# Decode attention with a gated MLP: whole batches in place of half batches, and half of the first key block turned on VectorE

## The chip, the cores and the metric

The kernel runs on one core of a Trainium2 chip. The core has a matrix engine (PE, TensorE), a vector engine (DVE, VectorE), an activation engine (ACT, ScalarE), a general engine (POOL, GpSimd) and a queue engine (SP, SyncE), and 16 load engines (DMA) that bring data from the chip's memory (HBM) into the on-chip buffer (SBUF). Matmul results land in a small accumulation memory (PSUM). Each engine works through its own instructions in order and waits on semaphores for the others. The metric is device time in microseconds; the kernel before takes 194.29 us (median of three runs, 194.04 to 194.38).

## What is computed

Eight sequences each decode one token of 448 features. An attention over the last 1024 cached positions (16 query heads, 8 key heads, 256 features a head) and an MLP (448 to 1792 to 448) run on the same token, and a sigmoid gate mixes them:

```python
q = (x @ wq).reshape(B, Sq, Hq, Dh).transpose(0, 2, 1, 3)
k = repeat(k_cache[:, :, Sk - W:, :], 2, axis=1)      # W = 1024
v = repeat(v_cache[:, :, Sk - W:, :], 2, axis=1)
p = softmax(einsum("bhqd,bhkd->bhqk", q, k) * Dh ** -0.5)
a = einsum("bhqk,bhkd->bhqd", p, v).transpose(0, 2, 1, 3).reshape(B, Sq, Hq * Dh) @ wo
h = gelu(layernorm(x) @ w1 + b1)
b = h @ w2 + b2
g = sigmoid((x * gate_w).sum(-1, keepdims=True))
return g * a + (1 - g) * b
```

All inputs are bfloat16. The used part of each cache is 33.5 MB; the weights add 10.6 MB.

## The kernel before

**Units.** A unit `u` is half a batch: 4 key heads of one sequence, 2 MB of keys and 2 MB of values; there are 16 units. One load puts a unit into a ring slot of 16 KB a partition: partition `32a + s` holds key head `a` and positions `32s` to `32s + 31`, so a partition reads one run of 16 KB. Only the first key load is cut in two pieces of 1 MB, with runs of 8 KB.

**The ring.** `plan` lists the loads in the order they are issued on SP: keys 0, w1, wq in two slots, w2, then keys and values in turn (values three units behind, `LAG`), and wo. The ring has `RING` = 9 slots. `pump()` issues loads while there are slots, and `done()` after the last use of a slot lets one more be issued; the load into a slot waits on the engine that read it last. Small inputs (x, gate weights, biases) are loaded on ACT's queue.

**A unit's work.** `transpose_keys(u)` turns the keys so that features lie on partitions: 32 PE transposes of 128x128 four-byte words (two bfloat16 each) into PSUM, four to a PSUM tile `ktp`, of which there are three; each tile is copied to `kt` in SBUF, four by ACT and four by VectorE (L349, L351). `scores(u)` does 32 matmuls into `S_ps`, one group of 32 partitions per key head; `top` takes the maximum on VectorE (L407). `expo`, `turn` and `bring` (exponential on ACT, 32x32 block transposes on VectorE, a permutation matmul) are called between the PSUM tiles of the next unit's transposes: `steps(u)` names after which. `values` does 16 matmuls into `PO`, and `finish` adds the parts with a small matmul and writes the head outputs to `oT`.

**Ends.** `norm_and_gate` comes first (layer norm of x, the gate, both turned on PE), then the transposes of unit 0, the MLP's hidden layer (`mlp_hidden`, 70 matmuls with w1 as the stationary operand), the queries, and the first scores. At the end `spread_rows` and `project` multiply the attention output with wo in 128 matmuls of 112 columns, and four stores write the result.

**Order.** The order is written by hand (`manual_schedule`); engines take their instructions as the functions are called. Waits follow from the tiles and from the pools: a tile of a pool with `bufs` buffers waits until a buffer's former tile is no longer read.

Of the kernel before, what the change touches and what calls it, by code (L numbers as in the profile page):

```python
# [17 lines left out]
def kernel(  # L18
# [15 lines left out]
    nc = tc.nc  # L34
# [10 lines left out]
    assert (NB, Sq, D, Hkv, Dh, Hq, W, F) == (8, 1, 448, 8, 256, 16, 1024, 1792)  # L45
    NJ = Dh // P
    NC = W // P
# [3 lines left out]
    NF = F // P  # L51
    FH = F // 2
    HH = HD // 2
    PAIR = 2
    OT = 4
    DO = D // OT
    QN = 512
    QUAD = 4
    RQ = QUAD * rep
    NQ = NB * Hkv // QUAD  # L60
    SK = P // QUAD
    NCK = W // SK
    NH = 2
    CH = NCK // NH
    SLOT = 8192
    CB = NC // NJ
    HPQ = 4
    NHQ = Hq // HPQ
    NJ8 = HPQ * NJ
    WO_PARTS = [[(0, NJ8)]] * (NHQ - 1) + [[(0, 4), (4, 6), (6, 8)]]  # L70
    RING = 9
    LAG = 3
    BIG = 1e30
# [8 lines left out]
    ktpool = ctx.enter_context(tc.tile_pool(name="ktpool", bufs=4))  # L82
    epool = ctx.enter_context(tc.tile_pool(name="epool", bufs=2))
    opool = ctx.enter_context(tc.tile_pool(name="opool", bufs=LAG + 1))
# [8 lines left out]
    consumed = [0]  # L93

# [10 lines left out]
    def kv_loader(src, u, parts):  # L105
        b, half = divmod(u, Hkv // QUAD)
        v = src[b, half * QUAD : (half + 1) * QUAD, kv_base:Sk, :].rearrange(
            "a (s c) d -> s a (c d)", c=NCK
        )

        def load(t):
            n = NCK * Dh // parts
            for i in range(parts):
                nc.sync.dma_start(  # L114
                    t[:, i * n : (i + 1) * n], v[:, :, i * n : (i + 1) * n]
                )

        return load

    def rows_loader(pieces):  # L120
        def load(t):
            o = 0
            for ap in pieces:
                n = 1
                for s in ap.shape[1:]:
                    n *= s
                dst = t[:, o : o + n]
                if len(ap.shape) == 3:
                    dst = dst.rearrange("p (a n) -> p a n", a=ap.shape[1])
                nc.sync.dma_start(dst, ap)  # L130
                o += n

        return load

    index = {}

    def add(key, loader):
        index[key] = len(plan)
        plan.append(loader)

    def add_kv(name, src, u, parts=1):
        add((name, u), kv_loader(src, u, parts))
# [5 lines left out]
    w2_v = B_w2.rearrange("(p c) n -> p (c n)", c=NF)  # L148
    wo_v = A_wo.rearrange("(q p j) n -> p q (j n)", p=P, j=NJ8)

    add_kv("k", A_k_cache, 0, parts=2)
    add(("w1",), rows_loader([w1_m, w1_t]))
    add(("wq", 0), rows_loader([wq_m[:, 0 : 2 * HD]]))
    add(("wq", 1), rows_loader([wq_m[:, 2 * HD : 3 * HD], wq_t]))
    add(("w2",), rows_loader([w2_v]))
    for u in range(1, NQ):
        add_kv("k", A_k_cache, u)
        if u >= LAG:
            add_kv("v", A_v_cache, u - LAG)
    for u in range(NQ - LAG, NQ):  # L160
        add_kv("v", A_v_cache, u)
    for q in range(0, NHQ, 2):
        add(
            ("wo", q),
            rows_loader(
                [
                    wo_v[:, q + i, j0 * D : j1 * D]
                    for i in range(2)
                    for j0, j1 in WO_PARTS[q + i]
                ]  # L170
            ),
        )

    def slot(*key):
        return slots[index[key]]

# [3 lines left out]
    gw_b = consts.tile([NB, D], BF16)  # L180
    b2_r = consts.tile([1, D], BF16)
    b1_sb = consts.tile([P, NF], BF16)
    nc.scalar.dma_start(
        gw_b[:], gate_w.rearrange("(o d) -> o d", o=1).to_broadcast([NB, D])
    )
    nc.scalar.dma_start(b2_r[:], B_b2.rearrange("(o d) -> o d", o=1))
    nc.scalar.dma_start(b1_sb[:], B_b1.rearrange("(p c) -> p c", c=NF))

# [4 lines left out]
    ones_f = consts.tile([P, P], F32)  # L193
    nc.gpsimd.memset(ones_f[:], 1.0)
# [3 lines left out]
    PO = ps_po.tile([P, PAIR, Dh], F32)  # L198
    nc.vector.memset(PO[:], 0.0)

    NX = NR + 2

    def tiles(ps):
        return [
            (ps[32 * i : 32 * i + NB, :], slice(i * DO, (i + 1) * DO))
            for i in range(OT)
        ]

    xz = consts.tile([NB, 2, P], BF16)
    yz = consts.tile([NB, 2, P], BF16)  # L210
    nc.vector.memset(xz[:], 0.0)
    nc.vector.memset(yz[:], 0.0)
    xT = consts.tile([P, NX, NB], BF16)
    yT = consts.tile([P, NX, NB], BF16)
    sel = consts.tile([P, RQ], F32)
    sel2 = consts.tile([P, RQ], F32)
    own = consts.tile([P, PAIR], F32)
    qw = consts.tile([P, NJ, NB, Hq // RQ, QUAD, RQ], BF16)
    oT = consts.tile([P, Hq, NJ, NB], BF16)
    gg = consts.tile([NB, 2], F32)  # L220
    spread = consts.tile([NB, OT, P // OT], F32)
    gg_s = consts.tile([P, 2], F32)
    ones_r = consts.tile([1, NB], BF16)
    mixb = consts.tile([P, DO], F32)
    res = consts.tile([P, DO], BF16)
    nc.vector.memset(spread[:], 0.0)
    nc.vector.memset(ones_r[:], 1.0)

    def transposed(dst, src, srcz):
        tp = ps_misc.tile([P, NX, NB], BF16, tag="misc", name="tp")  # L230
        for r in range(NR):
            nc.tensor.transpose(tp[:, r, :], src[:, r:DM:NR], ident[:NB, :NB])
        for h in range(2):
            nc.tensor.transpose(tp[:, NR + h, :], srcz[:, h, :], ident[:NB, :NB])
        nc.vector.tensor_copy(dst[:], tp[:])

    for h in range(2):
        nc.vector.tensor_copy(xz[:, h, h::2], x_sb[:, DM:D])
    transposed(xT, x_sb, xz)
    nc.vector.reduce_sum(  # L240
        sel[:], ident[:].rearrange("p (a s) -> p s a", a=QUAD)[:, 0:RQ, :], axis=AXIS.X
    )
    halfs = ident[:].rearrange("p (a s) -> p s a", a=QUAD)
    for i in range(PAIR):
        nc.vector.reduce_sum(
            own[:, i : i + 1], halfs[:, i * RQ : (i + 1) * RQ, :], axis=AXIS.XY
        )
    nc.vector.reduce_sum(
        sel2[:],
        ident[:]  # L250
        .rearrange("p (a h s) -> p s a h", a=QUAD, s=RQ)[:, :, :, 0:PAIR],
        axis=AXIS.XY,
    )
    perm = consts.tile([P, P], BF16)
    nc.vector.tensor_copy(
        perm[:].rearrange("p (s a) -> p s a", a=QUAD),
        ident[:].rearrange("p (a s) -> p s a", a=QUAD),
    )
    cap = consts.tile([P, 1], F32)
    rows = consts.tile([P, 1], F32)  # L260
    for a in range(QUAD):
        nc.vector.reduce_sum(
            rows[32 * a : 32 * a + 32, :],
            ident[32 * a : 32 * a + 32, (32 + rep) * a : (32 + rep) * a + rep],
            axis=AXIS.X,
        )
    nc.vector.tensor_scalar(
        cap[:], rows[:], 2.0 * BIG, -BIG, op0=ALU.mult, op1=ALU.add
    )
    nc.vector.memset(qw[:], 0.0)  # L270

    def norm_and_gate():
# [18 lines left out]
        for h in range(2):  # L291
            nc.vector.tensor_copy(yz[:, h, h::2], y_sb[:, DM:D])
        transposed(yT, y_sb, yz)
# [6 lines left out]
            in1=gw_b[:],  # L300
# [5 lines left out]
        nc.scalar.activation(gth[:], gl[:], ACT.Tanh, scale=0.5)  # L306
        nc.vector.tensor_scalar(
            gg[:, 0:1], gth[:], 0.5, 0.5, op0=ALU.mult, op1=ALU.add
        )
        nc.vector.tensor_scalar(  # L310
            gg[:, 1:2], gth[:], -0.5, 0.5, op0=ALU.mult, op1=ALU.add
        )
        nc.vector.tensor_copy(
            spread[:, :, 0:NB],
            ident[0:NB, 0:NB]
            .rearrange("p (o b) -> p o b", o=1)
            .to_broadcast([NB, OT, NB]),
        )
        gp = ps_misc.tile([P, 2], F32, tag="misc", name="gp")
        nc.tensor.matmul(  # L320
            gp[:],
            lhsT=spread[:].rearrange("p i b -> p (i b)"),
            rhs=gg[:],
# [3 lines left out]
        nc.vector.tensor_copy(gg_s[:], gp[:])  # L327

    KT = {}
    def transpose_keys(u, between=None):  # L330
        kn = slot("k", u)[:].bitcast(F32)
        between = between or {}
        for hf in range(NH):
            kt = ktpool.tile([P, QUAD, CH, SK, NJ], BF16, tag="kt", name="kt")
            KT[hf] = kt
            for i in range(CH // CB):
                c0 = i * CB
                g = hf * (CH // CB) + i
                ktp = ps_kt.tile([P, CB, P, NJ], BF16, tag="ktp", name="ktp")
# [12 lines left out]
                for step in between.get(g, ()):  # L352
                    step()
# [209 lines left out]
    for u in range(1, NQ):  # L563
        transpose_keys(u, steps(u - 1))
        if u >= LAG:
            values(u - LAG)
# [94 lines left out]
```

## Time and profile before

| What | Value |
|---|---|
| Median of three runs | 194.29 us |
| Span of the profiled execution, first to last instruction | 192.9 us (the page gives no further time for it) |
| Busy: PE, VectorE, ACT, POOL | 141.4, 121.4, 84.3, 1.3 us |
| Loads | 77.90 MB in 6737 packets, mean 404 GB/s |
| Mean granted PE clock | 0.907 of full |
| Chain that ended last | 96% loads |

The profile shows one execution. Its second part cuts the span into 40 slices of 4.8 us and gives, for each, an engine's busy tenths, the PE clock that was granted and the rate of the loads. The chain of waits goes back from the last instruction, at each step to what released it. A group's row gives the source line, engine, operation, output and input tiles, shapes, count, then total busy time and the mean of one in nanoseconds, then the idle time ahead of it and what ended most of that. In the list of waits a row gives the engine, what it waited for, total, times and longest in us; `SPq` and `ACTq` are the queues on which loads are issued. In a table of stretches, a row gives from and to, the length, the busy time and count of PE, PE's weight loads, VectorE, ACT and POOL, then the PE clock, the load engines' share and GB/s.

### The profile page before, as it was taken

Reading aid. Unit: us, or ns where it says so; the run is one execution under the profiler, and the core shown is the slowest. Engines: PE = TensorE matmul, PEld = TensorE weight load, DVE = VectorE, ACT = ScalarE, POOL = GpSimd, SP = SyncE. Lnnn points to the kernel's source line nnn. Section 1 sums busy time; section 2 is a strip of 40 time slices with the busy share of each in tenths; the row PEclk is TensorE's granted clock in tenths of the full one; section 3 lists DMA queues with packets and bytes.
Section 4 is the critical chain, followed back from the end, with each engine's and each line's share of the span. In section 5 each row is a group of like instructions: output and inputs, shape, how many; then the busy total and the mean of one; then the engine's idle time right before and its main releaser. Section 6 shows DMA issues by size and latency. Waiting matters only on the chain.

```text
span 192.9 us, 3529 instructions
## 1 busy us (share of the span) xinstructions
PE 141.4 (73%) x1478; PEld 104.7 (54%) x1478; DVE 121.4 (63%) x278; ACT 84.3 (44%) x102; POOL 1.3 (1%) x9
## 2 busy tenths in 40 slices
PE   1299957788888859797858586869786978935671
PEld 0199526465575649484636363739473948612360
DVE  7632335797987848576858676765867584863310
ACT  2343024587583817182818182827282725520000
POOL 2000000000000000000000000000000000000000
PEclk9999699999999997969999999996999696995558
DMA  5999999999999999999999999999999999999960
GB/s 173 426 427 415 429 440 423 404 431 431 431 431 421 425 418 425 435 426 428 425 418 431 416 431 428 428 428 421 428 428 421 428 431 425 428 418 413 417 240 7
DMA packets 6737, 77.90 MB, mean 404 GB/s; under 512 B 945, under 2 KB 1346, under 8 KB 1986
## 3 DMA queue, kind: packets, MB, share of 16 engines
q1 hardware_dynamic: 6512, 77.67, 95.5%
q8 instruction: 11, 0.18, 0.4%
q10 hardware_dynamic: 210, 0.02, 0.2%
q14 instruction: 4, 0.03, 0.0%
HBM read 77.68 MB, written 0.01 MB: 403 GB/s over the span
## 4 chain that ended last, share of the span: by engine, by line
DMA 96%; SPq 1%; issue 0%; DVE 0%; PE 0%
DMA slot<-in_A_k_cache_dram 58%; DMA slot<-in_A_v_cache_dram 21%; DMA slot<-in_A_wo_dram 10%; DMA slot<-in_A_wq_dram 7%; SPq L114 1%; SPq L130 1%; DVE res L620 0%; PE A_ps L604 0%
## 5 line engine op out<-in xcount | busy, mean ns | idle before, releaser
L343 PE MATMUL ktp<-ident_f,slot 128*128 128x128 f32 x512 | 78.0, 306 | 24.3 <-DMA slot<-in_A_k_cache_dram 16.0
L349 ACT COPY kt<-ktp 128x1024 bf16<-128x1024 bf16 x64 | 63.2, 1016 | 71.2 <-PE ktp L343 71.1
L343 PEld LDWEIGHTS ktp<-ident_f,slot 128*128 128x128 f32 x512 | 64.7, 157 | 33.6 <-issue 16.2
L351 DVE COPY kt<-ktp 128x1024 bf16<-128x1024 bf16 x64 | 41.8, 686 | 27.5 <-PE ktp L343 27.5
L423 DVE STREAM_TRANSPOSE EB<-E 128x1024 bf16<-128x1024 bf16 x16 | 19.9, 1243 | 5.9 <-ACT E L415 5.9
L407 DVE TENSOR_REDUCE nmx<-S_ps 128x1 f32<-128x1024 f32 x16 | 19.5, 1219 | 3.3 <-PE S_ps L395 3.3
L456 PE MATMUL PO<-slot,ET 128*16 128x512 bf16 x256 | 18.3, 410 | 2.1 <-DMA slot<-in_A_v_cache_dram 2.1
L395 PE MATMUL S_ps<-kt,qw 128*8 128x512 bf16 x256 | 18.2, 388 | 1.4 <-ACT kt L349 1.1
L415 ACT ACTIVATE E<-S_ps,nmx 128x1024 bf16<-128x1024 f32 x16 | 17.9, 1119 | 2.4 <-DVE nmx L408 2.4
L395 PEld LDWEIGHTS <-qw 128*8 128x8 bf16 x256 | 7.1, 85 | 8.8 <-issue 2.1
L456 PEld LDWEIGHTS <-ET 128*16 128x16 bf16 x256 | 5.4, 91 | 8.7 <-issue 5.4
L436 DVE CAST ET<-sm 128x256 bf16<-128x256 f32 x16 | 6.6, 415 | 0.7 <-PE sm L434 0.7
L434 PEld LDWEIGHTS sm<-selr,ones_f 128*128 128x128 f32 x32 | 5.0, 198 | 0.6 <-issue 0.4
L484 DVE CAST oT<-sm 128x16 bf16<-128x16 f32 x16 | 3.5, 219 | 2.9 <-PE sm L481 2.9
L434 PE MATMUL sm<-selr,ones_f 128*128 128x8 f32 x32 | 4.8, 222 | 0.0
L431 PE MATMUL sm<-EB,perm 128*128 128x256 bf16 x16 | 4.5, 279 | 0.3 <-DVE oT L484 0.3
L604 PE MATMUL A_ps<-slot,oP 128*8 128x112 bf16 x128 | 3.5, 273 | 1.1 <-DMA slot<-in_A_wo_dram 1.1
L514 DVE TENSOR_TENSOR z<-hT,b_sb 128x112 f32<-128x112 f32 x1 | 0.3, 274 | 5.5 <-PE hT L504 5.5
L604 PEld LDWEIGHTS <-oP 128*8 128x8 bf16 x128 | 2.7, 114 | 1.8 <-issue 1.8
L415 ACT ACTIVATION_READ_ACCUMULATOR E<-S_ps,nmx 128x1 f32 x16 | 3.2, 202 | 0.0
L363 PE MATMUL S_ps<-slot,xT 128*8 128x512 bf16 x32 | 3.2, 576 | 0.0
L438 DVE RECIPROCAL rb<-sm 128x8 f32<-128x8 f32 x16 | 3.2, 198 | 0.0
(145 smaller groups left out, 82.5 us busy)
## 6 DMA issues: line engine op xcount, KB each, us to landing
slot<-in_A_v_cache_dram SPq DMA_DIRECT2D x16, 2048.0 KB, 38.1
slot<-in_A_k_cache_dram SPq DMA_DIRECT2D x15, 2048.0 KB, 37.5
slot<-in_A_wo_dram SPq DMA_DIRECT2D x3, 896.0 KB, 31.8
slot<-in_A_k_cache_dram SPq DMA_DIRECT2D x2, 1024.0 KB, 7.4
slot<-in_A_wq_dram SPq DMA_DIRECT2D x1, 2048.0 KB
slot<-in_B_w_dram SPq DMA_DIRECT2D x1, 1568.0 KB
slot<-in_B_w_dram SPq DMA_DIRECT2D x1, 1344.0 KB, 10.1
slot<-in_A_wq_dram SPq DMA_DIRECT2D x1, 1024.0 KB
```

Source lines behind the costliest of these rows:

```text
L343: nc.tensor.transpose(words[:, c, :, 0], kn[:, o : o + P], ident_f[:])
L349: nc.scalar.copy(dst, src)
L351: nc.vector.tensor_copy(dst, src)
L395: nc.tensor.matmul(S_ps[32 * a : 32 * a + RQ, hf * CH * SK : (hf + 1) * CH * SK], lhsT=qw[:, j, b, half, a, :], rhs=KT[hf][:, a, :, :, j], ...
L407: nc.vector.reduce_max(nmx[:], S_ps[:], axis=AXIS.X, negate=True)
L415: nc.scalar.activation(E[:], S_ps[:], ACT.Exp, bias=nmx[:], scale=1.0, accum_out=rowsum[:])
L423: nc.vector.transpose(EB[:].rearrange("p c r -> p (c r)"), E[:])
L431: nc.tensor.matmul(sm[:, 0:NCK, :], lhsT=perm[:], rhs=EB[:, :, 0:RQ], start=True, stop=True)
L434: nc.tensor.matmul(sm[:, NCK, :], lhsT=ones_f[:], rhs=selr[:], start=True, stop=True)
L436: nc.vector.tensor_copy(ET[:], sm[:, 0:NCK, :])
L456: nc.tensor.matmul(PO[32 * t : 32 * t + PAIR * RQ], lhsT=ET[:, PAIR * c : PAIR * (c + 1), :], rhs=vn[:, PAIR * c * Dh : PAIR * (c + 1) * D ...
L604: nc.tensor.matmul(dst, lhsT=oP[:, j, q, :], rhs=w[:, o + cols.start : o + cols.stop], start=(q == 0 and j == 0), stop=(q == NHQ - 1 and j ...
```

## The change

The unit becomes a whole batch: 8 key heads, 4 MB of keys, two loads of 2 MB into one slot of 32 KB a partition, and the ring has 4 slots. wq takes one slot, w1 and w2 share one, wo takes one. The order of loads is keys 0, wq, w1 with w2, keys 1, then values and keys in turn, and wo. Each of `S_ps`'s groups of 32 partitions now holds four rows of scores, for two key heads, so a batch has one maximum and one exponential. The exponential writes four-byte floats and is turned together with its row sums; the scale 1/sum and the gate are multiplied in at once, and a mask made from the identity puts each head's weights in its columns. `softmax(b)` is called right after `scores(b)`, and then `values(b - 1)`, `bring(b)`, `finish(b - 1)`; nothing is called between the transposes any more. `finish` turns and adds on VectorE, without PE.

x, y, the queries and the MLP's hidden values are turned with VectorE's block transposes and small copies instead of PE transposes; biases and gate weights come as single rows and are spread by VectorE's shuffle. The MLP and projection matmuls have x and the attention output as stationary operand and the weights as moving operand with 448 (or 224) columns. Two stores write the result.

The first half of the keys of batch 0 (`turn_blocks(0, 0)`) is not turned by PE: VectorE turns it in 32x32 blocks into a tile `B`, and 16 copies of 32 partitions by 2048 elements, 6 on VectorE, 7 on ACT, 3 on POOL, bring the blocks to their partitions. `kt` and `B` share a pool of two buffers. TensorE has 2235 instructions for 2987.

```diff
-    SLOT = 8192
-    RING = 9
-    LAG = 3
+    HS = NCK * Dh
+    SLOT = NG * HS
+    RING = 4
+    EARLY = 16
-    ktpool = ctx.enter_context(tc.tile_pool(name="ktpool", bufs=4))
+    ktpool = ctx.enter_context(tc.tile_pool(name="ktpool", bufs=2))
...
+    add(("k", 0), kv_loader(A_k_cache, 0))
+    add(("wq",), rows_loader([wq_m, wq_t]))
+    add(("w12",), rows_loader([w1_m, w1_t, w2_v]))
+    add(("k", 1), kv_loader(A_k_cache, 1))
+    for b in range(2, NB):
+        add(("v", b - 2), kv_loader(A_v_cache, b - 2))
+        add(("k", b), kv_loader(A_k_cache, b))
...
+    for t in range(QD):
+        nc.scalar.dma_start(
+            b1_r[BL * t : BL * t + 1, :],
+            B_b1[FQ * t : FQ * (t + 1)].rearrange("(o d) -> o d", o=1),
+        )
...
+    nc.vector.stream_shuffle(b1_b[:], b1_r[:], [0] * BL)
...
+    def turn_blocks(b, hh):
+        kn = slot("k", b)[:].bitcast(F32)
+        kt = ktpool.tile([P, QD, NCK, SK, NJ], BF16, tag="kt", name="kt")
+        KT[hh] = kt
+        B = ktpool.tile([P, NCK, QD, SK // QD, QD, NJ], BF16, tag="kt", name="B")
+        n = NCK * P // QD
+        words = B[:].rearrange("p c w s a j -> p (c w s a j)").bitcast(F32)
+        for i in range(QD):
+            nc.vector.transpose(
+                words[:, i * n : (i + 1) * n],
+                kn[:, hh * NCK * P + i * n : hh * NCK * P + (i + 1) * n],
+            )
+        copies = [nc.vector.tensor_copy, nc.scalar.copy, nc.gpsimd.tensor_copy]
+        turn = [0, 1, 2, 1, 0, 1, 0, 2, 1, 0, 1, 2, 0, 1, 0, 1]
+        S8 = SK // QD
+        for w in range(QD):
+            for g in range(QD):
+                copies[turn[w * QD + g]](
+                    kt[BL * w : BL * (w + 1), :, :, g * S8 : (g + 1) * S8, :],
+                    B[BL * g : BL * (g + 1), :, w].rearrange("p c s a j -> p a c s j"),
+                )
...
+        qt = work.tile([P, 2, rep, QD, NJ, BL], BF16, tag="w3", name="qt")
+        nc.vector.transpose(
...
+        for i in range(QD):
+            for g in range(QD):
...
+                nc.vector.tensor_copy(dst, src)
...
+    def softmax(b):
+        nmx = spool.tile([P, 1], F32, tag="nmx", name="nmx")
+        nc.vector.reduce_max(nmx[:], S_ps[:], axis=AXIS.X, negate=True)
+        nc.scalar.activation(
+            E[:, 0:W], S_ps[:], ACT.Exp, bias=nmx[:], scale=1.0,
+            accum_out=E[:, W : W + 1],
+        )
+        EB = epool.tile([P, NCK + 1, BL], F32, tag="EB", name="EB")
+        nc.vector.transpose(EB[:].rearrange("p c r -> p (c r)"), E[:])
+        rs = spool.tile([P, BL], F32, tag="rs", name="rs")
+        nc.vector.stream_shuffle(rs[:], EB[:, NCK, :], [0] * BL)
...
-    norm_and_gate()
-    transpose_keys(0)
-    hs = mlp_hidden()
+    turn_blocks(0, 0)
+    transpose_keys(0, [1])
     query()
     scores(0)
-    top(0)
+    softmax(0)
+    hs = mlp_hidden()
+    bring(0)
     mlp_out(hs)
-    for u in range(1, NQ):
-        transpose_keys(u, steps(u - 1))
...
+    for b in range(1, NB):
+        transpose_keys(b)
+        scores(b)
+        softmax(b)
+        values(b - 1)
+        bring(b)
+        finish(b - 1)
...
+    for c in range(EARLY):
...
+    nc.sync.dma_start(out_f[:, 0:HALF], res[0:NB, :])
+    nc.scalar.dma_start(out_f[:, HALF:D], res[BL : BL + NB, :])
```

In `transpose_keys(b, halves)` ACT and VectorE copy the PSUM tiles in turn, ACT first, and `done()` follows the last half; `norm_and_gate` stands ahead of `turn_blocks` in the text, so on VectorE too.

## Prediction

> **What bounds the kernel now.** I read the page's chain, then the load rate by slice, then the queue's waits, and the instruction groups last, for prices. The chain that ended last is loads almost to the end:
>
> ```profile
> DMA 96%; SPq 1%; issue 0%; DVE 0%; PE 0%
> DMA  5999999999999999999999999999999999999960
> GB/s 173 426 427 415 429 440 423 404 431 431 431 431 421 425 418 425 435 426 428 425 418 431 416 431 428 428 428 421 428 428 421 428 431 425 428 418 413 417 240 7
> HBM read 77.68 MB, written 0.01 MB: 403 GB/s over the span
> ```
>
> The 16 load engines are full from the second slice to the last but two, at about 427 GB/s. Both kernels read the same 77.68 MB, which at that rate takes 181.9 us. The span of 192.9 holds that, 2.2 us before the first bytes, the slow ends and 3.5 us of tail. So a change gains little here, but whatever leaves the load queue empty is added in full. Next, who held back the loads, and the prices:
>
> ```profile
> SPq L114 <- DMA slot<-in_A_k_cache_dram: 44.7, 13, 5.2
> SPq L114 <- PE ktp L343: 14.0, 11, 3.9
> SPq L114 <- DMA b_sb<-in_B_b_dram: 1.6, 1, 1.6
> ...
> L349 ACT COPY kt<-ktp 128x1024 bf16<-128x1024 bf16 x64 | 63.2, 1016 | 71.2 <-PE ktp L343 71.1
> L351 DVE COPY kt<-ktp 128x1024 bf16<-128x1024 bf16 x64 | 41.8, 686 | 27.5 <-PE ktp L343 27.5
> L423 DVE STREAM_TRANSPOSE EB<-E 128x1024 bf16<-128x1024 bf16 x16 | 19.9, 1243 | 5.9 <-ACT E L415 5.9
> L407 DVE TENSOR_REDUCE nmx<-S_ps 128x1 f32<-128x1024 f32 x16 | 19.5, 1219 | 3.3 <-PE S_ps L395 3.3
> L415 ACT ACTIVATE E<-S_ps,nmx 128x1024 bf16<-128x1024 f32 x16 | 17.9, 1119 | 2.4 <-DVE nmx L408 2.4
> masks.py:199 POOL TENSOR_SCALAR_AFFINE_SELECT ident<-ident 128x128 bf16<-128x128 bf16 x1 | 0.3, 292 | 0.1
> ```
>
> SP's queue mostly waits for older loads to land, up to 39 us after their issue: far ahead. It also waits for PE to release a slot, and that wait is still covered. In order of time, the queue and the small loads at the start:
>
> ```profile
> 1.98 0.37 ACTq L187 DMA_DIRECT2D b_sb<-in_B_b_dram  x1
> ...
> 9.31 3.42 SPq L114 DMA_DIRECT2D slot<-in_A_k_cache_dram  x3
> ...
> 12.78 0.60 SPq L114 DMA_DIRECT2D slot<-in_A_v_cache_dram  x1
> ```
>
> A 3.5 KB load issued at 1.98 us held SP until 9.31: beside the large loads a small one lands up to 7.3 us late. Last, stretches of time, with PE's clock and the load engines' share at the end of each line:
>
> ```profile
> 175.00:185.00 10.00, 6.21 (x62) 3.23 (x65) 3.32 (x11) 0.00 (x0) 0.00 (x0) 0.50 0.99 409
> 187.00:188.00 1.00, 0.86 (x32) 0.72 (x32) 0.00 (x0) 0.00 (x0) 0.00 (x0) 0.62 0.14 52
> 188.00:189.00 1.00, 0.55 (x24) 0.36 (x24) 0.00 (x0) 0.00 (x0) 0.00 (x0) 1.00 0.05 20
> ```
>
> **The change, part by part.**
>
> *Load stream.* Rows of 8 KB become 16 KB only in the first key load; the other key and value rows had 16 KB already. In the first full microseconds the rate was 318 and 393 GB/s for 427 later: at most 0.3 us to gain. TensorE's code comes over queue q8, 11 packets with 0.4% of 16 engines' span, so 12.3 us of engine time, 1.1 each. With 2235 instructions for 2987, in proportion, three go: 0.2 us if spread over all engines, 3.4 if one engine, the last, had all three. After 187 us the load engines are busy 14% and then 5%, so one or two finish late. I take 0.7 us. Together minus 1.0, between 0 and minus 3.7. [...]
>
> *What leaves PE.* The small transposes of x and y, the matmuls that build selections and sums, 70 hidden matmuls for 14, 128 projections of 112 columns for 16 of 448 and 32 of 224: all lay beside loads that end later, so they are worth nothing here. Two stores for four save one issue on each queue, half of SP's 0.71, and the wider last sum gives some of it back: 0.2, left out.
>
> *When the first key slot is released, R0.* Four ring slots of 4 MB replace nine of 2 MB. The first four loads (keys 0, wq, w1 with w2, keys 1) are 15.27 MB: at 427 GB/s from 2.2 us on, the queue is dry at 38.0 us unless the values of batch 0 are issued before. They wait for slot 0, so for the last PE transpose of keys 0. That transpose is late:
> - VectorE is in order, and the norm and gate chain stands ahead of the block turning. Its memsets and placings end at about 4.5 us. Then it needs b1, four one-row loads on ACT's queue, the last issued near 3.4 us; landing 1.5 (as x did) to 7.3 us later is 4.9 to 10.7. I take 9, nearest the b1 row, and 0.6 for the shuffle: 9.6.
> - From there to the end of the preamble: masks 0.6; from BatchNorm statistics to y 1.7 as before; placing 0.65; a transpose of 1280 elements, scaled from 1243 ns, 1.5; copies 0.6; gate product 0.7 and tanh 0.3; spreading the gate 1.7. Sum 7.8: 17.4 us (13.3 to 19).
> - Four transposes of 128x1024 words by the 1243 ns row: 5.0, at 17.4 to 22.4. The row is bf16, these are f32: 5.0 to 10.
> - Sixteen copies of 32x2048, each needing all four transposes. ACT has seven: L349 is 1016 ns for 1024 elements; doubled that is 2.03, and with 297 ns for the 112 elements of L529 as the fixed part's measure 1.83; I take 1.87 each, 13.1. VectorE has six, 0.7 to 1.4 each by L351, so 4 to 8, under ACT. POOL has three; its only reading row is 292 ns for 128 elements: between 0.3 (all of it fixed) and 4.7 (all of it per element), so 1 to 14 in all. I take ACT as last: 35.5.
> - The second half's PSUM copies go into a `kt` buffer that is free only after all sixteen (`ktpool` has two: `kt`, `B`). So PE stops after three of eight PSUM tiles, and the other five take 3.7 more through ACT and VectorE at 1.01 and 0.69. R0 = 39.2 us (35 to 45).
>
> [...]
>
> *When the weight slot is released, M.* From R0 on PE: query matmuls 3.8 (32 took 3.2, four more across the array); ACT copy and VectorE transpose 2.5; sixteen small copies at 0.18, 2.9; scores 2.1 (16 took 1.08); softmax 5.0 (1.22, 1.12+0.2, 1.28, four small ones); memset and hidden matmuls 1.7; nine VectorE and ACT steps on 448 columns, scaled from 0.27 at 112, 5.0; output matmuls 14 x 0.2 to 0.37, 3 to 5. Sum 27 (24 to 29): M = 66.2. Values 1 wait for this slot. Values 0 and keys 2 cover 19.6 us after the first dry point, so with no stall the queue would be dry at 57.6; the load is on its way 1.4 us after M, 67.6. So loads lose 10.0 us in two stalls, 2.6 at slot 0 (38.0 to 40.6) and 7.4 at the weight slot (60.2 to 67.6). Work used to hide this: before, the keys came in 2 MB pieces, the queue held nine, and PE transposed them as they landed.
>
> *The batch loop.* Per batch: transposes paced by ACT's eight copies (8 x 1.01) behind two VectorE steps left over from the batch before, 10.3; rest of the scores 1.0; softmax 5.4, of which the value matmuls cover 2.1; bring 0.3: 17.0, and 17.4 with a little of the lower clock. A batch of loads takes 19.6. The softmax was hidden inside the next transposes and is now open; the halved count of maxima and exponentials (8 for 16) pays part. So the loop doesn't bound, and PE, late at M, catches up 2.2 us a batch.
>
> *The end.* Loads: 192.9 + 10.0 - 1.0 = 201.9. PE: batch 7 starts at 66.2 + 6 x 17.4 = 170.6; then transposes and scores 11.6, softmax 5.4, bring and mask 1, values at half clock 3, finish 2, projection 4, the last sum and the store 3.5: 201.1. The two ends nearly meet, the later one counts, and either can slip: 202.1 of span. Outside the span lie 1.4 us (the median of three runs is 194.29; the page gives no other time for the profiled one): 203.5.
>
> **The rivals.**
> 1. *The queue never runs dry.* For: the loop has 2 us of slack a batch, and the stream itself is no longer than before. Against: it needs M before 56, so R0 before 29, which ACT's seven copies alone forbid unless VectorE's preamble ended by 7 us. Then 192.9 - 1.0 + 1.4 = 193.3, between 190.6 and 194.3. This is the other side, and R0 = 29 is the point from which it decides.
> 2. *Only a small stall.* b1 lands early (4.9), R0 = 35, short M: M = 59 and 2.8 to 6 us lost: 196 to 200.
> 3. *POOL's copies or the loop are worse than my rows.* POOL at 15 to 20 us for three (VectorE and POOL copying at the same time) makes R0 41 to 46; or the loop takes 19.6 a batch because PE, idle 3 us in each, gets half the clock (0.50 was granted at 175 to 185 us, where PE waited), which puts batch 7 at 184 and the end at 214. Together 208 to 216.
>
> **How the numbers follow.** Mine 0.52 at 203.5, its own range 200 to 208. Rival 1 0.11, rival 2 0.19, rival 3 0.18. Leaving out most of rival 1 and the upper part of rival 3, the range is 195 to 212. A difference under 0.2% can't be told from none. Rival 1 is nearly all faster (0.10), 0.02 in the band, slower 0.88.
>
> **What would show it.** Load rate down in slice 9 of 40 (about 38 to 41 us) and slices 13 and 14 (60 to 68), 427 elsewhere; SP's queue waiting there for PE, not for loads. ACT's seven copies of 32x2048 at 1.87 back to back from about 22 us, and PE's second-half transposes standing behind them. Batch cycles of 17 to 18 us after 66. q8 with eight packets. If no slice under 400 shows between 30 and 70 us, rival 1 holds and my chain is wrong, most likely in VectorE's preamble or in the copies; if POOL ends after ACT, or the cycle is over 19, it is rival 3.

## Result, and the profile after

The changed kernel takes 220.52 us (median of four, 219.68 to 220.92) where the kernel before takes 194.18: a ratio of 1.135 (95% interval 1.1325 to 1.1374). I forecast 203.5, with a range of 195 to 212. The direction was right, the size was not: the loss is 26 us where I had 9. The profiled execution took 219.68 us and spans 217.8. Medians here and in the table below are over all runs of a kernel; the ratios leave out single runs that lay far above the others of the same kernel (218.3 us with b1 spread later, 293.4 with the three together, 240.5 with the kernel before).

The second and fourth parts of the page: 40 slices of 5.445 us, and the chain that ended last.

```profile
PEclk9999999997665699979969957995899999599587
DMA  6999999089980089999999999999999999999700
GB/s 233 425 448 415 420 429 430 8 313 433 433 361 3 0 313 433 424 427 418 427 427 427 429 430 433 417 415 424 430 424 430 433 433 424 421 412 412 275 0 1
...
PE 34%; DVE 27%; ACT 16%; issue 3%; ACTq 0%; DVEq 0%
```

The loads have two holes, near 38 to 49 us and near 60 to 82. Against 427 GB/s they lose 6.8 us in the first ((419 + 114) / 427 x 5.445) and 13.1 in the second: 19.9 us, twice my 10.0. And loads are no longer in the chain at all, where they were 96% of it: the last two slices, 11 us, have no loads (the kernel before has one such slice, 5 us).

The queue's waits, in total, times and longest, and then its issues in order of time:

```profile
SPq L115 <- PE ktp L332: 91.4, 7, 18.7
SPq L115 <- PE bb L543: 28.6, 1, 28.6
...
SPq L115 <- DVE B L308: 12.7, 1, 12.7
```

```profile
43.41 1.18 SPq L115 DMA_DIRECT2D slot<-in_A_v_cache_dram  x2
46.28 1.18 SPq L115 DMA_DIRECT2D slot<-in_A_k_cache_dram  x2
76.19 1.18 SPq L115 DMA_DIRECT2D slot<-in_A_v_cache_dram  x2
```

So slot 0 was released at 43.4 (my R0: 39.2), and the weight slot, by the last output matmul of the MLP (`bb`), at 76.2 (my M: 66.2). What led there, on VectorE, then ScalarE and GpSimd (start, length, and in brackets the wait before it):

```profile
11.29 0.01 DVE L209 LOAD_MASK_SELECT b_b<-b_r  x1 [3.35 <-DMA b_r<-in_B_b_dram]
...
20.02 4.61 DVE L308 STREAM_TRANSPOSE B<-slot 128x1024 f32<-128x1024 f32 x4
24.66 11.19 DVE L317 COPY kt<-B 32x2048 bf16<-32x2048 bf16 x6
```

```profile
24.66 13.35 ACT L317 COPY kt<-B 32x2048 bf16<-32x2048 bf16 x7 [6.46 <-DVE B L308]
...
46.29 4.70 ACT L371 ACTIVATE qs<-S_ps 128x1024 bf16<-128x1024 f32 x1 [2.72 <-PE S_ps L361]
```

```profile
24.77 8.12 POOL L317 COPY kt<-B 32x2048 bf16<-32x2048 bf16 x3 [21.64 <-DVE B L308]
```

and on TensorE:

```profile
38.84 4.53 PE L332 MATMUL ktp<-ident_f,slot 128*128 128x128 f32 x20 [22.69 <-DVE kt L340]
43.30 1.96 PE L349 MATMUL S_ps<-slot,xw 128*8 128x512 bf16 x24
...
55.22 3.37 PE L399 MATMUL S_ps<-kt,qw 128*4 128x512 bf16 x32 [8.97 <-DVE qw L391]
64.01 1.29 PE L496 MATMUL hp<-slot,xw 128*8 128x448 bf16 x12 [5.43 <-DVE hp L491]
...
71.70 4.46 PE L543 MATMUL bb<-slot,hs 128*8 128x448 bf16 x14 [5.39 <-DVE hs L530]
```

Until 76 us TensorE mostly waits: 22.7 us for a `kt` buffer, 9.0 for the queries, 5.4 for the softmax, 5.4 for the MLP's hidden values. Then the loop. One batch's scores, the values of the batch before and the wait for the softmax look like this; below them are that wait in total over the kernel, and the first transposes of batch 1 and of batch 7:

```profile
102.73 2.00 PE L399 MATMUL S_ps<-kt,qw 128*4 128x512 bf16 x32
104.54 1.92 PE L461 MATMUL PO<-slot,ET 128*16 128x512 bf16 x32
109.70 0.27 PE L436 MATMUL sm<-EZ,perm 128*128 128x128 bf16 x1 [3.24 <-DVE EZ L425]
```

```profile
PE sm L436 <- DVE EZ L425: 22.7, 7, 3.2
```

```profile
76.09 1.53 PE L332 MATMUL ktp<-ident_f,slot 128*128 128x128 f32 x12
...
183.06 1.62 PE L332 MATMUL ktp<-ident_f,slot 128*128 128x128 f32 x12
```

TensorE waits 3.2 us in each batch for the softmax. Batch 1 starts at 76.1 us and batch 7 at 183.1, so 17.8 us a batch; the end follows 34.7 us after that.

### The profile page after: what moved, and what is told of

Same layout as the page of the kernel before. It is cut to its first block, busy times and chain, and to the rows that moved or that the text cites. A ratio compares the mean times of both kernels' runs of the same rounds, so it can differ in the third digit from the quotient of the medians.

```text
span 217.8 us, 2745 instructions
## 1 busy us (share of the span) xinstructions
PE 121.2 (56%) x1104; PEld 83.6 (38%) x1104; DVE 133.3 (61%) x267; ACT 90.9 (42%) x89; POOL 10.5 (5%) x15
## 4 chain that ended last, share of the span: by engine, by line
PE 34%; DVE 27%; ACT 16%; issue 3%; ACTq 0%; DVEq 0%
PE ktp L332 19%; ACT kt L338 10%; PE S_ps L399 8%; DVE EB L418 5%; DVE nmx L412 5%; ACT E L413 4%; DVE oP L482 3%; ACT qs L371 2%; PE bb L543 2%; DVE T L472 2%; PE PO L461 2%; DVE kt L340 2%; DVE ET L444 2%; DVE qw L391 1%; DVE acc L587 1%
## 5 line engine op out<-in xcount | busy, mean ns | idle before, releaser
L332 PEld LDWEIGHTS ktp<-ident_f,slot 128*128 128x128 f32 x480 | 64.1, 164 | 74.8 <-issue 33.4
L338 ACT COPY kt<-ktp 128x1024 bf16<-128x1024 bf16 x60 | 59.7, 1013 | 47.2 <-PE ktp L332 46.7
L399 PE MATMUL S_ps<-kt,qw 128*4 128x512 bf16 x256 | 17.4, 412 | 9.0 <-DVE qw L391 9.0
L413 ACT ACTIVATE E<-S_ps,nmx 128x1024 f32<-128x1024 f32 x8 | 8.9, 1114 | 29.9 <-DVE nmx L412 29.9
L412 DVE TENSOR_REDUCE nmx<-S_ps 128x1 f32<-128x1024 f32 x8 | 9.8, 1224 | 11.5 <-PE S_ps L399 11.5
L418 DVE STREAM_TRANSPOSE EB<-E 128x1056 f32<-128x1056 f32 x8 | 10.2, 1278 | 10.6 <-ACT E L413 10.6
L317 ACT COPY kt<-B 32x2048 bf16<-32x2048 bf16 x7 | 13.3, 1898 | 6.5 <-DVE B L308 6.5
L436 PE MATMUL sm<-EZ,perm 128*128 128x128 bf16 x8 | 2.0, 247 | 22.7 <-DVE EZ L425 22.7
L399 PEld LDWEIGHTS <-qw 128*4 128x4 bf16 x256 | 6.7, 86 | 17.1 <-issue 10.6
L317 DVE COPY kt<-B 32x2048 bf16<-32x2048 bf16 x6 | 11.1, 1854 | 0.1
L482 DVE TENSOR_TENSOR oP<-Y 32x32 bf16<-32x32 f32 x32 | 9.4, 294 | 1.1
L317 POOL COPY kt<-B 32x2048 bf16<-32x2048 bf16 x3 | 8.0, 2678 | 21.7 <-DVE B L308 21.6
L472 DVE STREAM_TRANSPOSE T<-PO 128x512 f32<-128x512 f32 x8 | 5.7, 707 | 1.5 <-PE PO L461 1.5
```

The costliest lines, as they stand in the source:

```text
L317: copies[turn[w * QD + g]](kt[BL * w : BL * (w + 1), :, :, g * S8 : (g + 1) * S8, :], B[BL * g : BL * (g + 1), :, w].rearrange("p c s a j ...
L332: nc.tensor.transpose(words[:, c, :, 0], kn[:, o : o + P], ident_f[:])
L338: nc.scalar.copy(dst, src)
L399: nc.tensor.matmul(S_ps[BL * t : BL * t + UR, n * QN : (n + 1) * QN], lhsT=qw[:, j, b, t, rep * u : rep * u + UR], rhs=KT[u][:, t, n * CQ ...
L412: nc.vector.reduce_max(nmx[:], S_ps[:], axis=AXIS.X, negate=True)
L413: nc.scalar.activation(E[:, 0:W], S_ps[:], ACT.Exp, bias=nmx[:], scale=1.0, accum_out=E[:, W : W + 1],)
```

## The theories, and the experiments

*Theory A*, formed from this profile: TensorE's chain sets the time. It is M, then six batches, then the end, and nothing before M can be made up, because the loop and the end have no slack. In the changed kernel the span is M + 141.6 us. *Rival B*: the lost load time sets it, so that each microsecond of a hole costs one. *Rival C*: the block turning is a small part, and the loop is the cause.

The table gathers what the profiles of the runs show. Slot 0 and M are the times at which SP issues the first values and the values of batch 1. "Six batches" runs from the maximum of batch 1 to that of batch 7. "Lost" is the load time lost in slices clearly under 427 GB/s, without the first slices and those in which the loads end. Each row's times from slot 0 on are of one profiled execution.

| Kernel | Median, us | Ratio to before (95%) | Slot 0 | M | Six batches | Lost | Span | Span - M |
|---|---|---|---|---|---|---|---|---|
| changed | 220.5 | 1.135 (1.1325-1.1374) | 43.4 | 76.2 | 110.4 | 19.9 | 217.8 | 141.6 |
| whole block on TensorE | 206.0 | 1.061 (1.0554-1.067) | 27.9 | 61.1 | 110.9 | 4.5 | 203.2 | 142.1 |
| queries in rows | 217.5 | 1.120 (1.1158-1.1244) | 43.1 | 73.1 | 111.8 | 18.2 | 216.4 | 143.3 |
| block turning first | 217.0 | 1.123 (1.1153-1.1297) | 31.8 | 74.9 | 108.8 | 18.6 | 215.0 | 140.1 |
| loop interleaved | 214.8 | 1.107 (1.1027-1.112) | 43.2 | 76.8 | 101.7 | 21.3 | 213.5 | 136.7 |
| the three together | 196.3 | 1.011 (1.0071-1.0138) | 28.5 | 58.6 | 100.1 | 2.1 | 194.2 | 135.6 |
| b1 spread later | 213.7 | 1.100 (1.0968-1.1026) | 39.0 | 72.6 | 108.0 | 16.3 | 211.7 | 139.1 |
| copies without GpSimd | 217.0 | 1.117 (1.1103-1.1233) | 41.1 | 74.8 | 108.0 | 18.7 | 214.0 | 139.2 |
| early release | 194.0 | 0.9996 (0.9981-1.0011) | 19.9 | 45.9 | 109.8 | 0 | 191.9 | 146.0 |
| early release, split end | 193.8 | 0.9981 (0.9973-0.999) | 19.4 | 46.0 | 110.4 | 0 | 191.8 | 145.8 |
| early release, block turning | 197.1 | 1.015 (1.0134-1.0171) | 33.0 | 58.6 | 101.3 | 2.8 | 195.6 | 137.0 |

**Undo the block turning.**

```diff
-    turn_blocks(0, 0)
-    transpose_keys(0, [1])
+    transpose_keys(0)
```

> TensorE turns the whole first key block, as for all later batches; no block turning and no sixteen copies. Theory A (TensorE's late chain sets the time: release of the weight slot, M, then six batches of about 18.2 us, then a tail of 32 us): slot 0 is released near 30 us for 43.4, M moves from 76.2 to about 63, and the time falls by the same 13 us to about 207. Theory B (the loads set it: what the queue loses is added to the end of the loads): of the 19.5 us that the loads lost, about 13 go, the loads end near 192, and the time is about 197 to 201. Theory C (the block turning is only a small part, the loop is the cause): 217 to 220.5.

206.0 us: 14.5 us of the 26.3 are the block turning's. The queue, and the rates:

```profile
27.91 1.19 SPq L115 DMA_DIRECT2D slot<-in_A_v_cache_dram  x2
30.30 1.18 SPq L115 DMA_DIRECT2D slot<-in_A_k_cache_dram  x2
61.09 1.18 SPq L115 DMA_DIRECT2D slot<-in_A_v_cache_dram  x2
```

```profile
GB/s 208 436 450 391 438 437 419 434 416 422 435 177 303 419 410 422 435 429 426 429 429 419 431 422 422 432 424 422 426 432 419 429 432 422 419 417 412 171 3 1
```

M fell by 15.1 us and the span by 14.6. The loads regained 15.4 us too, so the gain alone does not tell A from B. The end does: the loads end in the slice from 188 to 193 us (the 171), as B has it, but the time is not B's 197 to 201: two more slices, 10 us, follow without loads, where the kernel before has one of 5 us. Rival C falls.

**Write the queries in rows.** In the changed kernel ScalarE reads the queries from PSUM in order and writes the two members of each pair of neighbours (`j`) to two different rows of 32 elements, 64 bytes apart. Now it writes in order and reads PSUM at a step of two elements.

```diff
-            qs[:].rearrange("p m j e -> p m e j"),
-            S_ps[:].rearrange("p (m e j) -> p m e j", e=BL, j=NJ),
+            qs[:],
+            S_ps[:].rearrange("p (m e j) -> p m j e", e=BL, j=NJ),
```

> ScalarE writes the scaled queries in rows without gaps and reads PSUM with the stride in its place; nothing else changes. The instruction took 4.70 us where I had summed 1.02. If the strided two-byte write is what cost, it takes 1.0 to 1.4 us now, M falls from 76.2 to about 72.6, and by theory A (M sets the time) the whole is about 217.0. If the strided read costs as much, or if the step is hidden, 220.5.

The one instruction, in this run and in the changed kernel (shortest, median and longest in ns):

```profile
L371 ACT ACTIVATE qs<-S_ps x1: 1023/1023/1023, 45.5 to 45.5; 128x1024 bf16<-128x1024 f32 x1
```

```profile
L371 ACT ACTIVATE qs<-S_ps x1: 4702/4702/4702, 46.3 to 46.3; 128x1024 bf16<-128x1024 f32 x1
```

It is the order of the write: with the reordering on the PSUM read in its place, the instruction took 1.02 us, like ScalarE's other copies of 128x1024 (L338, 1.01 us each). M fell by 3.1 us, the time by 3.0. (The spans of the two profiled executions differ by 1.4 only; the six batches, which this edit does not touch, took 1.4 more in this one.) So an instruction that is 3.7 us shorter on the chain ahead of M is worth nearly that at the end.

**Turn the blocks ahead of the norm.** The definitions and the calls move; nothing else does.

```diff
+    turn_blocks(0, 0)
+    transpose_keys(0, [1])
+
     place(xs[0:NB, 0], x_sb)
...
-    turn_blocks(0, 0)
-    transpose_keys(0, [1])
     query()
```

> The block turning is kept, but stands on VectorE ahead of the norm and gate chain, so the late b1 rows no longer hold it. Theory A: slot 0 is released near 32 us for 43.4 and the first stall of the loads is gone, but the turned x is ready only near 42 us, the queries are no earlier, M stays at 75 to 76 and the time at 219 to 220.5. Theory B (the lost load time is added to the end): 6.5 us less, about 214.

This run was meant to part A from B, since it takes the first hole away and leaves M. Rates, and the queries' wait for the turned x:

```profile
GB/s 245 425 428 417 422 428 430 439 419 421 335 0 0 0 326 436 430 418 430 430 430 427 416 430 433 428 406 433 433 424 418 433 430 427 427 421 410 362 18 1
```

```profile
40.25 2.73 PE L352 MATMUL S_ps<-slot,xw 128*8 128x512 bf16 x24 [8.51 <-DVE xw L297]
```

Slot 0 came free 11.6 us earlier and the first hole is gone, but the second took it over: 18.6 us lost for 19.9. M moved by 1.3. The time, 217.0, lies between the two forecasts, 2 us under A's and 3 above B's. Of the 2.8 us that the span fell, 1.3 are M and 1.6 the six batches (108.8 for 110.4), which this edit does not touch. With the lost time down by 1.3 only, both theories ask for 1.3, so the run does not part them after all. It shows that taking away the first hole gives nothing while M stays, and A's number was 2 us off for the pace of the loop, of which below.

**Interleave the loop.** The softmax is cut after the exponential; its second part, `bring` and the `finish` of the batch before are called between the PSUM tiles of the next batch's transposes.

```diff
     for b in range(1, NB):
-        transpose_keys(b)
...
+            steps = {
+                3: [lambda: turn(b - 1)],
+                7: [lambda: bring(b - 1)],
+                10: [lambda: finish(b - 2)],
+            }
+        transpose_keys(b, between=steps)
         scores(b)
-        softmax(b)
+        top(b)
         values(b - 1)
-        bring(b)
-        finish(b - 1)
+    turn(NB - 1)
+    bring(NB - 1)
+    finish(NB - 2)
```

> Only the loop changes: after the maximum and the exponential the rest of the softmax, bring and finish of a batch stand between the PSUM tiles of the next batch's transposes. M stays at 76.2. Theory A, with the loop as the second part of the loss: a batch takes TensorE 13 to 15 us, it catches up with the loads, which end near 205 as before, and the time is about 210. If only M and the stalls count and the loop was never short of time: 220.

```profile
110.18 0.22 PE L441 MATMUL sm<-EZ,perm 128*128 128x128 bf16 x1 [0.81 <-DVE EZ L430]
```

```profile
GB/s 238 424 430 422 427 428 430 66 258 430 436 424 28 0 147 417 381 411 433 427 424 431 424 424 427 427 422 430 430 414 433 430 420 427 433 427 411 412 282 1
...
PE 26%; DMA 25%; DVE 17%; ACT 10%; issue 2%; SPq 0%; DVEq 0%; ACTq 0%
```

The wait for the softmax falls to 0.8 us and the first batches take 15.3 us; by batch 6 TensorE has caught up with the loads and waits for them (21.0 and 19.1). 214.8 us, against 210 forecast. Here B holds: the loads are all but over at 207 us (61 GB/s in the microsecond after it, none from 208 on), with 21.3 us lost, where I had 205, and 6.5 us follow, where I had reckoned with 3. So the loop and the holes are the two ceilings, a few microseconds apart: the loop taken away alone gains 5.7 us, and then the holes hold the time.

**The three together.**

> The whole first block on TensorE, the queries written without gaps, and the interleaved loop, together. If M and the loop together are the loss: M near 57.5 us, the queue loses 1 to 2 us for 21, TensorE's loop (15.3 us a batch where the loads allowed it) runs ahead of the loads, the loads end near 187 and the tail after them is 6.6 us as in the run with the interleaved loop alone: span 194, time about 196. If the effects overlap so that only the largest counts: 206.

196.3 us, as forecast. Two of the edits gain 14.5 and 3.0 alone, the third 5.7; together they gain 24.2 (their sum is 23.2). What is left is a hole of 2.1 us and the longer end.

**Spread b1 later.** Only the shuffle at L209 moves.

```diff
     b1_b = consts.tile([P, FQ], BF16)
-    nc.vector.stream_shuffle(b1_b[:], b1_r[:], [0] * BL)
...
     turn_blocks(0, 0)
     transpose_keys(0, [1])
+    nc.vector.stream_shuffle(b1_b[:], b1_r[:], [0] * BL)
     query()
```

> Only the shuffle that spreads b1 moves, from ahead of the masks and the norm to behind the copies of the first key block; VectorE no longer waits 3.35 us for the b1 rows ahead of the block turning. If the small load is on the chain as I forecast: slot 0 is released 4 us earlier (39.4), M is 72.2 and the time 216.5. If something else would hold VectorE there anyway (the keys, the identity from POOL, the tanh on ScalarE): 219 to 220.5.

```profile
16.10 4.61 DVE L307 STREAM_TRANSPOSE B<-slot 128x1024 f32<-128x1024 f32 x4
20.74 11.21 DVE L316 COPY kt<-B 32x2048 bf16<-32x2048 bf16 x6
```

The turning starts 3.9 us earlier, slot 0 and M follow by 4.4 and 3.6. So four loads of 0.9 KB that land late are paid in full when an engine whose next work is on the chain has to wait for them. The time fell by 6.8, more than M did: 2.4 of it is again the six batches (108.0).

**Copies without GpSimd.** VectorE takes ten of the sixteen copies, ScalarE six.

```diff
-        copies = [nc.vector.tensor_copy, nc.scalar.copy, nc.gpsimd.tensor_copy]
-        turn = [0, 1, 2, 1, 0, 1, 0, 2, 1, 0, 1, 2, 0, 1, 0, 1]
+        copies = [nc.vector.tensor_copy, nc.scalar.copy]
+        turn = [0, 1, 0, 0, 1, 0, 1, 0, 0, 1, 0, 1, 0, 0, 1, 0]
```

> The sixteen copies are shared by VectorE (10) and ScalarE (6); POOL has none. In the changed kernel VectorE's copies took 1.00, 1.87 and 2.68 us for the same shape while POOL copied beside it at 2.68 each. If POOL's copying is what slowed VectorE's: ten copies at 1.00 take 10 us, ScalarE's six 11.4, the copies end 1.9 us earlier, and the time is about 218.6. If VectorE needs 1.86 in the mean by itself: 18.6 us for its ten, 5 us later than before, and the time is about 225.

The copies of the changed kernel, then of this run:

```profile
L317 ACT COPY kt<-B x7: 1893/1895/1914, 24.7 to 36.1; 32x2048 bf16<-32x2048 bf16 x7
L317 DVE COPY kt<-B x6: 1005/1872/2685, 24.7 to 34.8; 32x2048 bf16<-32x2048 bf16 x6
L317 POOL COPY kt<-B x3: 2660/2663/2712, 24.8 to 30.2; 32x2048 bf16<-32x2048 bf16 x3
```

```profile
L317 DVE COPY kt<-B x10: 1002/1007/1092, 24.7 to 34.1; 32x2048 bf16<-32x2048 bf16 x10
L317 ACT COPY kt<-B x6: 1893/1896/1906, 24.7 to 34.3; 32x2048 bf16<-32x2048 bf16 x6
```

Ten copies of VectorE alone take less time (10.4 us) than six beside GpSimd (11.2). GpSimd's three copies cost VectorE three copies of 2.7 us for 1.0. What frees slot 0 earlier, by 2.3 us (1.9 forecast), is that ScalarE, the last to end, has one copy less. M fell by 1.4 us; the time is 217.0, and 2.4 us of its gain are the six batches (108.0).

**Release the slots early.** On top of the three together: only what the norm of x needs stands ahead of the first block; the shuffles, masks and the gate follow later; the MLP is finished before the second part of the first softmax.

```diff
-    nc.vector.stream_shuffle(b1_b[:], b1_r[:], [0] * BL)
...
-    gall, oall, b2s = norm_and_gate()
+    norm()
...
     transpose_keys(0)
...
+    nc.vector.stream_shuffle(b1_b[:], b1_r[:], [0] * BL)
...
     query()
+    gall, oall, b2s = gate()
     scores(0)
     top(0)
-    turn(0)
     hs = mlp_hidden()
-    bring(0)
     mlp_out(hs)
```

> As the run of the three together, and beside it only what the norm of x needs stands ahead of the first key block on VectorE and ScalarE; biases, masks and the gate follow later, and the MLP is finished before the rest of the first softmax, so the weight slot is released near 45 us and slot 0 near 20. If the stalls of the queue are then the last loss: no slice of the load rate is under 400 between 10 and 180 us, the loads end near 186, and with the tail of 6.6 us the span is 192.3 and the time about 194.2. If TensorE is still the bound after M: 200 or more.

```profile
GB/s 217 428 417 466 388 438 400 427 430 437 434 430 403 427 434 427 434 427 413 425 427 434 423 427 423 422 423 430 434 420 427 427 417 434 430 427 407 421 271 2
...
DMA 53%; PE 20%; DVE 18%; ACT 5%; issue 2%; SPq 0%; DVEq 0%; ACTq 0%
```

No hole is left (the 388 and 400 stand beside 466 and 438), and the time is that of the kernel before: 0.9996 (0.9981 to 1.0011). M has become free: it is 12.7 us earlier than with the three together, and the span only 2.3; the six batches now take 109.8 us, because TensorE waits for the loads in them. Once the loads are the bound, only the holes count.

**The block turning put back into it.**

```diff
-    transpose_keys(0)
+    turn_blocks(0, 0)
+    transpose_keys(0, [1])
```

> As the run with the early release of the slots, with the block turning put back (half of the first block on VectorE and sixteen copies). If the turning costs its chain wherever it stands: VectorE is free for it near 11 us, four transposes and the copies on ScalarE bring slot 0 to about 33 and M to about 59; the queue loses 0 to 3 us at the weight slot and the time is 194 to 197. If it was the preamble ahead of it alone that made it late: slot 0 near 20 and 194.0.

```profile
33.01 1.18 SPq L115 DMA_DIRECT2D slot<-in_A_v_cache_dram  x2
36.06 1.18 SPq L115 DMA_DIRECT2D slot<-in_A_k_cache_dram  x2
58.63 1.18 SPq L115 DMA_DIRECT2D slot<-in_A_v_cache_dram  x2
```

197.1 us, 3.1 more, at the upper edge of the 194 to 197 forecast. Even with only the norm of x in front of it, the turning brings slot 0 to 33.0 us for 19.9, so the preamble was not alone at fault; in this surrounding most of it is hidden, because M at 58.6 is only just too late (2.8 us lost).

**Split the end.** The last batch's values are multiplied and finished by key-head half, and the first sixteen projection matmuls follow the first half.

```diff
-    values(NB - 1)
-    finish(NB - 1)
...
+    for u in range(NG):
+        values_half(NB - 1, u)
+    done()
+    for u in range(NG):
+        finish_half(NB - 1, u, T7, Y7)
```

> As the run with the early release of the slots, and the end cut in halves: the values of the last batch are multiplied and finished by key-head half, so that the first half's share needs only the first piece of the last value load, and the first sixteen projection matmuls and their four additions lie beside the second half. If the tail after the loads (5 us there) is VectorE's and TensorE's chain from the last values: the last sum stands about 0.5 us after the last weight piece, 1.5 to 2 us earlier, and the time is 192.0 to 192.5, under the kernel before. If the tail is the last pieces of the load itself: 194.

```profile
186.07 2.75 PE L644 MATMUL A<-slot,oP 128*8 128x224 bf16 x32 [1.21 <-DMA slot<-in_A_wo_dram]
```

```profile
188.86 0.38 DVE L659 TENSOR_TENSOR res<-A,fin 40x224 bf16<-40x224 f32 x1 [0.30 <-PE A L644]
```

193.8 us, 0.19% under the kernel before, with an interval just short of 1, so about what can be told from no change; 1.5 us of gain were forecast, and 0.2 came. TensorE now waits for the last pieces of wo, as the second half of the expectation has it. The last two landed at 187.7 and 188.3 us, while without the split the last one landed at 186.9 and the projection's matmuls, wo's last readers, ended at 187.5. This kernel has 32 matmuls more, but as many packets of code on q8, nine; what delayed the last pieces was not tried.

## Why the prediction was wrong

*Right.* The holes, their two places and their releasers (a late slot 0 and a late weight slot, both waiting for TensorE); ScalarE's copies at 1.87 (1.895 measured) as the last of the three engines; the order of what stands ahead of the block turning; q8's eight packets, as this row has them:

```profile
q8 instruction: 8, 0.13, 0.2%
```

The rival in which the queue never runs dry, at 193.3 us when slot 0 is free before 29 and M before 56, is what the run with the early release shows: 19.9, 45.9, and 194.0 us. On the gain of the load stream I took 1.0 between 0 and 3.7: in that run the load engines moved nothing after 187 us, where in the kernel before they worked until 189, so at most about 2. That execution of the kernel before is itself some 0.5 long (it spans 192.9 us; twelve later runs of the same kernel have a median of 192.4), 5 us follow the loads for 4, and the time fell by 0.2 at most. Longer rows, code and slow ends were not told apart.

*Wrong: the sum of TensorE's chain*, 201.1 us forecast and 217.8 measured. The steps are there, and nearly every one is longer:

| Step of the prediction | Forecast | Measured | Difference |
|---|---|---|---|
| b1 spread | 9.6 | 11.9 | +2.3 |
| preamble, transposes, ScalarE's copies | 25.9 | 26.1 | +0.2 |
| the other five PSUM tiles | 3.7 | 5.4 | +1.7 |
| query matmuls | 3.8 | 2.9 | -0.9 |
| ScalarE's copy and VectorE's transpose of the queries | 2.5 | 6.0 | +3.5 |
| small copies, scores | 5.0 | 6.4 | +1.4 |
| first softmax | 5.0 | 4.8 | -0.2 |
| hidden matmuls and nine steps | 6.7 | 8.3 | +1.6 |
| output matmuls | 4 | 4.5 | +0.5 |
| six batches | 104.4 | 107.0 | +2.6 |
| batch 7 to the end | 30.5 | 34.7 | +4.2 |

(M is 10.0 us late; the rows up to it add up to 10.1 by rounding. The 17.0 us between 203.5 and 220.5 are these 16.7, less the 1.0 that I had added for the meeting of the two ends, and 1.3 more: 1.9 us outside the span for 1.4, and a profiled execution 0.8 under the median.) The largest miss on the way to M is the queries' copy, priced by copies of the same size: it writes the two members of each pair 64 bytes apart, and no row of ScalarE in the profile before had that. For the landing of b1 I had bounds of 4.9 to 10.7, and VectorE waited for it until 11.3, above them. The rest is nearly all TensorE's pace. I had priced its matmuls by rows of a kernel in which, after the first 10 us, it is never idle for more than 2.4 us at a time; here it stands idle for 5 to 23 us and then works slowly, and these stretches lie on the chain: the five tiles (421 ns a transpose after 22.7 us), the first scores (628 ns a matmul after 9.0 us, 387 in the loop), the hidden and the output matmuls (577 and 574 ns a matmul after 5.4 us each). At the end it is the transposes of batch 7: with the scores they took 14.4 us for 11.6. I had the slow pace in the last values, at 3 (3.6 measured), and 0.4 us a batch for it in the loop.

*The larger error is one of structure.* I wrote that "the two ends nearly meet" at 201.9 and 201.1, and that TensorE catches up 2.2 us a batch (1.8 measured: 17.8 where the loads take 19.6). With my M that was so. From there on each further microsecond at M was 1 us of time, as the first two experiments showed, and that I did not carry into the range: my upper end came from GpSimd's copies or a loop of 19.6, and neither came about (GpSimd ended 5 us before ScalarE, and a batch took 17.8 us). The bounds of M alone (45 + 29 = 74) would have led to 74 + 104.4 + 30.5 + 1.4 = 210.3, those of M and the loop together to 223.5. I had put them into separate cases, as if they excluded each other.

No run shows the 15 to 20 us that the third rival gave to GpSimd's three copies: they took 8.1 us, from 24.8 to 32.9, at 2.66 to 2.71 each with VectorE copying beside them, and 8.2 in the run with the early release and the block turning.

## What to carry to other kernels

A late start is hidden only as long as something later has slack, so follow the first release of every buffer of a short ring to the end, and add the bounds of all steps on that chain rather than choose one. Ahead of the first release an engine's program should hold only what that release needs: here a bias row, a gate and a mask stood in front of 4 MB of keys. A share of the work given to an idle engine must be weighed against whom that engine disturbs: here GpSimd's three copies stretched three of VectorE's from 1.0 to 2.7 us.

## What the runs showed that I had not expected

- *ScalarE's write in jumps.* 1024 two-byte elements a partition, in pairs whose second member is written 64 bytes behind the first, took 4.70 us; the same instruction with the reordering on the PSUM read took 1.02. Other distances were not tried.
- *VectorE's and GpSimd's copies end in turn.* While both copied, three of VectorE's copies of 32x2048 lasted 2.69 us each and GpSimd's three 2.66 to 2.71. VectorE's last two, behind GpSimd's end at 32.9 us, took 1.00 each, and its ten in the run without GpSimd 1.007. The ends alternate: one of VectorE's about 0.93 us after one of GpSimd's, and one of GpSimd's about 1.77 after one of VectorE's. So 1.7 of VectorE's 2.69 us were there only beside GpSimd; how the two come to alternate, these rows do not show. What GpSimd's copy takes with VectorE idle, no run shows.
- *TensorE was slow after the pauses ahead of M, and the granted clock does not show it every time.* After 22.7 us of waiting, 20 transposes lasted 421 ns each (median); in the loop, from 98.8 to 102.5 us, it was 273. The first two lines are the rows of those two stretches, the third the granted clock of the first (third number from the end): it reads 1.00. It does read 0.62 from 71.7 to 76.2 us, where the output matmuls are slow (574 ns for 448 columns; the loop's scores, of 512, take 387).

```profile
L332 PE MATMUL ktp<-ident_f,slot x20: 421/421/477, 38.8 to 43.0; 128*128 128x128 f32 x20
```

```profile
L332 PE MATMUL ktp<-ident_f,slot x27: 272/273/329, 98.8 to 102.5; 128*128 128x128 f32 x27
```

```profile
38.80:43.40 4.60, 4.55 (x24) 4.23 (x28) 1.38 (x2) 3.07 (x4) 0.00 (x0) 1.00 0.01 2
```

  So here the duration of a known matmul told more than the granted clock. The slow stretches also go with the time of the six batches, 108.0 to 111.8 us in kernels that do not differ there: of their 384 transposes, 74 lasted over 380 ns in both runs with 108.0, and 86, 99, 122 and 134 in those with 108.8, 110.4, 110.9 and 111.8. What decides where they fall stays open. Differences of 2 us between the runs above are therefore read from M, not from the time.
